# RWKV-5 time mixing and a SwiGLU block: chunks of 64 tokens with one score product per head, and y with channels on partitions

## The chip, the core and the metric

The kernel runs on one core of one Trainium2 chip. A core has a matrix engine (PE; its weight loads are shown as PEld), three engines for elementwise work (DVE, ACT, POOL) and SP, which issues the transfers here. Each takes its instructions in order. The metric is the device time of one execution in microseconds.

## What is computed

Time mixing over 4 batches, 8 heads, 768 tokens and 48 channels, then a feed-forward block with an RMS norm over 3,072 tokens, 384 features and 1,536 hidden units. Everything is float32, except that the three weight matrices arrive as float64.

```python
state = np.zeros((B, H, D, D), dtype=np.float32)
for t in range(S):
    kt, vt, rt = (k[:, :, t], v[:, :, t], r[:, :, t])
    cur = np.einsum('bhd,bhe->bhde', u[None] * kt, vt)
    y[:, :, t] = np.einsum('bhd,bhde->bhe', rt, state + cur)
    state = w[None, :, :, None] * state + np.einsum('bhd,bhe->bhde', kt, vt)
x = np.ascontiguousarray(y.transpose(0, 2, 1, 3)).reshape(B * S, H * D)
xn = x / np.sqrt(np.mean(x * x, axis=-1, keepdims=True) + 1e-06) * rms_g
g = xn @ w_gate
out = (g * (1.0 / (1.0 + np.exp(-g))) * (xn @ w_val)) @ w_out
```

`w` is drawn between 0.85 and 0.95.

## The kernel before

**Time mixing** goes chunk by chunk: 128 tokens of one batch, 24 chunks. `r` and `k` lie with channels on partitions, two heads to a tile (rows 0-47 and 64-111). The scores A[t,j] = sum of r[t] k[j] w^(t-1-j) over j < t are built in seven levels (halves of 64, 32, ..., 1 tokens), so that no power of w is negative: `prep` (L253) multiplies k by falling powers on POOL (L259) and r by rising ones on DVE (L264), `levels` (L279) has one product for each level and head (L292), even heads into one PSUM bank and odd heads into the other, and DVE copies the masked part of each level into `AT` (L300; the largest half by ACT, L297). `outputs` (L308) forms r.(uk) (L315), k-hat times v for the state (L322), r w^t times the state (L329) and A times v (L335), adds them on DVE and takes the sum of squares on ACT. The result has tokens on partitions.

**Feed-forward** works on blocks of three chunks, 384 tokens. `transposes` turns x (L378); `gate_val` (L386) makes for each of 12 hidden tiles two products of three matmuls (L393), a sigmoid on ACT (L397) and two multiplications on DVE (L398, L399); `project` (L401) adds 12 products for 128 tokens (L406) and ACT copies the result out (L410). Matmuls in float32 appear as two passes, so as two records.

**Weights** are rounded to float32 in 36 pieces of 128 x 384 by `round_piece` (L161): six operations on DVE (L176 to L187) and an addition on POOL (L188). `rounded` puts this ahead of the first product that needs a piece.

**Order.** The source interleaves steps of the feed-forward part of the block before (`todo`, `step`) with the mixing of the present chunk; a scheduler then fixes each engine's order from dependences, priorities and free buffers. PSUM has two tiles for the levels, two for gate and value and two for all else (projections among it).

Of the kernel before, what the change touches and what calls it, by code (L numbers as in the profile page):

```python
# [13 lines left out]
"""  # L14
# [14 lines left out]
FP32 = mybir.dt.float32  # L29
# [4 lines left out]
ALU = mybir.AluOpType  # L34
PSUM = bass.MemoryType.PSUM

P = 128
L = 128
EPS = 1e-6


def free_dims(t, *dims):
# [5 lines left out]
def tile_rwkv5_then_swiglu(  # L48
    ctx: ExitStack,
    tc: tile.TileContext,  # L50
    rT: bass.AP,  # [B, H, D, S]
    kT: bass.AP,  # [B, H, D, S]
    k: bass.AP,  # [B, S, H, D]
    v: bass.AP,  # [B, S, H, D]
    w: bass.AP,  # [H, D]
    u: bass.AP,  # [H, D]
    w_gate: bass.AP,  # [DM, DFF]
    w_val: bass.AP,  # [DM, DFF]
    w_out: bass.AP,  # [DFF, DM]
    rms_g: bass.AP,  # [DM]  # L60
    out: bass.AP,  # [B * S, DM]
):
    nc = tc.nc

# [11 lines left out]
    WQ = 4  # L76
# [59 lines left out]
    # The weights in float32. Given in float64 (its bits, as int64), they are rounded here, piece by piece.  # L136
# [67 lines left out]
    # masks[s][j, q, i]: whether j is in the left half of block q (of 2s tokens), whose right half's tokens are i  # L204
# [13 lines left out]
    # powers of w by doubling: up[n] = w^n, down[n] = w^(L-1-n), wL = w^L  # L218
# [14 lines left out]
    # w^(L-1-t) with tokens on partitions  # L233
# [19 lines left out]
    def prep(n):  # L253
        """What chunk n needs of r, k and the powers of w."""
# [24 lines left out]
    def levels(n, two):  # L279
        """A^T of chunk n for one or two sizes of halves; one bank for the even heads, one for the odd."""  # L280
# [27 lines left out]
    def outputs(n):  # L308
        """Chunk n's rows of x, the sums of their squares, and the next state."""
# [131 lines left out]
    while todo:  # L441
        step()


# [26 lines left out]
```

## Time and profile before

| | us |
|---|---|
| median of three runs | 947.51 (947.07 to 949.36) |
| span of the profiled execution, first to last instruction | 943.5 |
| gate products L393 (pg), busy | 217.6 |
| value products L393 (pv), busy | 201.6 |
| projections L406, busy | 198.9 |
| score products L292, busy | 164.2 for the levels by R and K |
| masked copies L300 on DVE, busy | 130.5 |
| powers times k, L259 on POOL, busy | 125.7 |

The page gives a span; the execution's own time is not listed apart from the runs', and 4.0 us lie between its span and their median. A row of a group reads: line, engine, operation, output and inputs by the program's names, tile shapes, count, then busy us, the mean of one in ns, and the idle time ahead of them with what ended it. In the timeline a row is a run of equal instructions: start, duration, engine, line, operation, count, and in brackets a wait ahead of it. In the slices a digit is a busy share in tenths.

### The profile page before, as it was taken

The numbers are of one execution on the slowest core, as the hardware profiler recorded it, in microseconds if no ns is written. First come the engines' busy times: TensorE is split into PE (matmuls) and PEld (weight loads), VectorE is DVE, ScalarE is ACT, GpSimd is POOL, SyncE is SP. The second block draws the span as 40 slices with busy tenths as digits, with TensorE's granted clock in tenths as the row PEclk, the third lists the DMA queues.
The fourth block names the chain that finished last, engine by engine and source line by source line (L and its number), as shares of the span: only waits on it lengthen the run. The fifth ranks groups of instructions, "written<-read, shape, count | busy, mean of one in ns | idle before, by whom it ended". The sixth has DMA issues, their size and how long they took to land.

```text
span 943.5 us, 13386 instructions
## 1 busy us (share of the span) xinstructions
PE 897.9 (95%) x5548; PEld 619.5 (66%) x5548; DVE 483.1 (51%) x874; ACT 121.9 (13%) x241; POOL 241.4 (26%) x291
## 2 busy tenths in 40 slices
PE   4776999979999999999999999999999999999998
PEld 4776766646667667766667667766667667766554
DVE  8999999972454435542455334542455334431220
ACT  0000211001211121101211121101211121102110
POOL 9864544450123112211123112211123110000000
PEclk9999999968999999999999999999999999999999
DMA  7343333110100101100100101100100100000000
GB/s 210 109 120 107 86 91 101 56 46 25 52 14 21 43 17 34 34 17 26 43 25 19 42 17 34 34 17 28 41 17 9 35 18 1 1 1 26 1 0 26
DMA packets 36556, 38.81 MB, mean 41 GB/s; under 512 B 4112, under 2 KB 31888, under 8 KB 36496
## 3 DMA queue, kind: packets, MB, share of 16 engines
q1 hardware_dynamic: 36496, 37.96, 14.0%
q8 instruction: 44, 0.72, 0.3%
q14 instruction: 16, 0.13, 0.0%
HBM read 33.23 MB, written 4.72 MB: 40 GB/s over the span
## 4 chain that ended last, share of the span: by engine, by line
PE 82%; DVE 13%; POOL 2%; issue 1%; DMA 1%; ACT 0%; SPq 0%; POOLq 0%; ACTq 0%; DVEq 0%
PE pg L393 20%; PE po L406 20%; PE pv L393 18%; PE pp L292 14%; PE Y L335 4%; PE Y L329 3%; DVE AT L300 2%; PE su L315 2%; DVE R L264 1%; DVE t L187 1%; PE su L322 1%; DVE t L182 1%; DVE t L186 1%; PE px L378 1%; POOL wo L188 1%
## 5 line engine op out<-in xcount | busy, mean ns | idle before, releaser
L393 PE MATMUL pg<-xT,wg 128*128 128x384 f32 x576 | 217.6, 516 | 2.1 <-DVE h L398 2.1
L406 PE MATMUL po<-wo,h 128*128 128x384 f32 x576 | 198.9, 501 | 6.1 <-POOL wo L188 5.7
L393 PE MATMUL pv<-xT,wv 128*128 128x384 f32 x576 | 201.6, 486 | 0.0
L259 POOL TENSOR_TENSOR K<-kT,down 128x256 f32<-128x256 f32 x144 | 125.7, 882 | 276.2 <-PE pp L292 271.3
L292 PEld LDWEIGHTS pp<-R,K 48*128 48x128 f32 (+1 forms) x2304 | 149.0, 201 | 59.4 <-issue 44.3
L292 PE MATMUL pp<-R,K 48*128 48x64 f32 (+1 forms) x2304 | 164.2, 291 | 18.6 <-DVE AT L300 16.6
L406 PEld LDWEIGHTS po<-wo,h 128*128 128x128 f32 x576 | 109.0, 194 | 80.2 <-POOL wo L188 8.4
L393 PEld LDWEIGHTS pv<-xT,wv 128*128 128x128 f32 x576 | 109.8, 191 | 77.3 <-issue 1.4
L393 PEld LDWEIGHTS pg<-xT,wg 128*128 128x128 f32 x576 | 106.1, 196 | 64.7 <-issue 6.6
L300 DVE COPY_PREDICATED AT<-mask,pp 128x512 f32<-128x512 int32 x144 | 130.5, 906 | 34.8 <-PE pp L292 28.3
L398 DVE TENSOR_TENSOR h<-pg,h 128x384 f32<-128x384 f32 x96 | 53.4, 557 | 139.5 <-ACT h L397 139.4
L264 DVE TENSOR_TENSOR R<-rT,up 128x256 f32<-128x256 f32 x144 | 66.9, 480 | 83.7 <-PE pp L292 82.9
L397 ACT ACTIVATE h<-pg 128x384 f32<-128x384 f32 x96 | 47.2, 491 | 337.1 <-PE pg L393 331.6
L399 DVE TENSOR_TENSOR h<-pv,h 128x384 f32<-128x384 f32 x96 | 53.4, 556 | 66.6 <-PE pv L393 66.6
L335 PE MATMUL Y<-v,AT 128*128 128x48 f32 x384 | 60.4, 289 | 3.1 <-DVE AT L300 3.1
L335 PEld LDWEIGHTS Y<-v,AT 128*128 128x128 f32 x384 | 56.8, 215 | 4.6 <-DVE AT L300 3.4
L275 POOL TENSOR_TENSOR khat<-k,wk 128x384 f32<-128x384 f32 x20 | 21.5, 1076 | 148.3 <-PE su L322 148.3
L329 PE MATMUL Y<-S,Rin 128*128 128x96 f32 x160 | 38.0, 323 | 0.0
L271 POOL TENSOR_TENSOR Rin<-rT,up 128x512 f32<-128x512 f32 x20 | 26.2, 1310 | 38.9 <-PE Y L329 38.0
L410 ACT COPY o<-po 128x384 f32<-128x384 f32 x24 | 11.5, 479 | 189.8 <-PE po L406 189.8
L297 ACT COPY AT<-pp 64x512 f32<-64x512 f32 x24 | 13.9, 581 | 151.9 <-PE pp L292 151.9
L315 PEld LDWEIGHTS su<-u,rk 128*128 128x128 f32 x192 | 28.2, 214 | 7.6 <-DVE rk L273 2.0
(69 smaller groups left out, 496.1 us busy)
## 6 DMA issues: line engine op xcount, KB each, us to landing
k<-in_k_dram SPq DMA_DIRECT2D x24, 192.0 KB, 2.4
kT<-in_kT_dram SPq DMA_DIRECT2D x48, 96.0 KB, 2.3
rT<-in_rT_dram SPq DMA_DIRECT2D x48, 96.0 KB, 2.5
v<-in_v_dram SPq DMA_DIRECT2D x24, 192.0 KB, 2.4
raw<-in_w_gate_dram SPq DMA_DIRECT2D x12, 384.0 KB, 3.8
raw<-in_w_val_dram SPq DMA_DIRECT2D x12, 384.0 KB, 3.8
raw<-in_w_out_dram SPq DMA_DIRECT2D x12, 384.0 KB, 3.1
out_dram<-o SPq DMA_DIRECT2D x24, 192.0 KB, 1.9
```

Of the source, the lines that this page charges most:

```text
L259: nc.gpsimd.tensor_mul(halves(kd, s, 0) if s < L // 2 else kd.rearrange("p a (q s) -> p a q s", s=s), halves(k_, s, 0), free_dims(down[:, ...
L264: nc.vector.tensor_mul(Rs[s][n % 2].rearrange("p a (q s) -> p a q s", s=s), halves(r_, s, 1), free_dims(up, (L, HP), (0, q), (1, s)),)
L292: nc.tensor.matmul(pp[0:M, e * HP + hc, i, :], lhsT, rhs, start=True, stop=True, skip_group_check=True)
L300: nc.vector.copy_predicated(halves(AT, s, 1), free_dims(masks[s], (0, H), (s, q), (1, s)), pp[:, :, i, :].rearrange("p a (q s) -> p a q s" ...
L315: nc.tensor.matmul(du[:, 2 * hc : 2 * hc + 2], rk[n][:, hc, :], u2[:, hc, :], start=True, stop=True, skip_group_check=True)
L329: nc.tensor.matmul(Y[:, 2 * hc : 2 * hc + 2, :].rearrange("p a d -> p (a d)"), R_in[n][:, hc, :], Sb[:, hc, :], start=True, stop=False, sk ...
L335: nc.tensor.matmul(Y[:, h, :], AT[:, e * HP + hc, :], vn[:, h * D : (h + 1) * D], start=c == 0, stop=True, skip_group_check=True,)
L393: nc.tensor.matmul(ps_, wt[:, cc, o * P : (o + 1) * P], xT[:, cc, :], start=cc == 0, stop=cc == CC - 1)
L397: nc.scalar.activation(h, pg, AF.Sigmoid)
L398: nc.vector.tensor_mul(h, pg, h)
L399: nc.vector.tensor_mul(h, pv, h)
L406: nc.tensor.matmul(po, hT[nn][:, j * P : (j + 1) * P], wo[i][:, o, :], start=nn == 0, stop=nn == NN - 1)
```

## The change

A new function `fast` does all of the work where each w lies in 0.5 to 1.5; the kernel of before stays as `general`, behind a branch on a count of the channels in that range.

* A chunk is 64 tokens of **all four batches**: 12 chunks. Powers of w are centred: r is multiplied by w^(t-32) and k by w^(31-j), so one product of 48 x 64 by 64 per head and batch gives all scores. Even heads use rows 0-47 and write partitions 64-127, odd heads the reverse; both go to one PSUM bank.
* `ME` (even heads) and `MO` (odd) hold r w^t in 48 rows and the scores in the other 64, with r.(uk) put on the diagonal by POOL. `VS` holds the state in the same 48 rows and v in the other 64. One product over 128 rows gives y with **channels on partitions**, so the transposes go. The fourth pair of heads is spread over rows 48-63 and 112-127 of the three feature tiles, by products of its own into the same columns.
* `KH` holds the diagonal of w^64 and k-hat, so one product gives the next state; ACT copies it into the next `VS`.
* The mean of squares comes from a product with a matrix of ones, over 256 tokens.
* Feed-forward blocks are 256, 256, then five times 512 tokens.
* Weights come in 24 pieces of 128 x 576: four operations on DVE, one on ACT, one on POOL.
* PSUM: four tiles for gate and value, three for mixing, one for projections.

```diff
+    ps_gv = ctx.enter_context(tc.tile_pool(name="ps_gv", bufs=4, space=PSUM))
+    ps_at = ctx.enter_context(tc.tile_pool(name="ps_at", bufs=3, space=PSUM))
+    ps_o = ctx.enter_context(tc.tile_pool(name="ps_o", bufs=1, space=PSUM))
...
+    def round_piece():
...
+            nc.scalar.activation(ulp, lo, AF.Copy, scale=2.0**-29)
+            mi = mag.bitcast(I32)
+            nc.vector.tensor_single_scalar(out=mi, in_=hi, scalar=0x7FFFFFFF, op=ALU.bitwise_and)
+            nc.vector.tensor_single_scalar(out=mag, in_=mag, scalar=2.0**-15, op=ALU.max)
+            nc.vector.tensor_scalar(
+                out=mi, in0=mi, scalar1=3, scalar2=0x3FFFFFF8, op0=ALU.logical_shift_left, op1=ALU.bitwise_and
+            )
+            nc.vector.scalar_tensor_tensor(
+                out=mi, in0=hi, scalar=-0x40000000, in1=mi, op0=ALU.bitwise_and, op1=ALU.bitwise_or
+            )
+            nc.gpsimd.tensor_tensor(out=dst.bitcast(I32), in0=mi, in1=ulp, op=ALU.add)
...
+    def prep(s):
...
+        nc.vector.tensor_mul(kc, ch[:, 1], table(down))
+        nc.vector.tensor_mul(me[0:D], ch[0:D, 0], table(up[0:D]))
+        nc.vector.tensor_mul(mo[64 : 64 + D], ch[64 : 64 + D, 0], table(up[64 : 64 + D]))
+        if s + 1 < NS:
+            load_chan(s + 1)
+        rk = one.tile([P, B, HP, D], FP32, name=f"rk_{s}", tag="rk")
+        nc.gpsimd.tensor_mul(rk, TOK[:, 0], TOK[:, 1])
+        nc.gpsimd.tensor_mul(rk, rk, free_dims(utab, (0, B), (D, HP), (1, D)))
+        du = work.tile([P, B * HP], FP32, name=f"du_{s}", tag="du")
+        nc.vector.tensor_reduce(out=du, in_=rk.rearrange("p b h d -> p (b h) d"), op=ALU.add, axis=AX.X)
+        for t, rows in ((me, slice(64, 128)), (mo, slice(0, 64))):
+            nc.gpsimd.tensor_mul(
+                t[rows].rearrange("p b h t -> p (b h) t"),
+                free_dims(dmask[rows], (0, B * HP), (1, L)),
+                free_dims(du[rows], (1, B * HP), (0, L)),
+            )
...
+    def scores(s, half):
...
+                for rows, to, m in ((slice(0, D), slice(64, 128), me), (slice(64, 64 + D), slice(0, 64), mo)):
+                    nc.tensor.matmul(
+                        pa[to, bl, p, :], kc[rows, b, p, :], m[rows, b, p, :], start=True, stop=True,
+                        skip_group_check=True,
+                    )
+        for to, m in ((slice(64, 128), me), (slice(0, 64), mo)):
+            nc.vector.copy_predicated(
...
+    def outputs(s, half):
...
+                for z, m in ((0, me), (1, mo)):
+                    nc.tensor.matmul(
+                        py[64 * z : 64 * z + 64, i, cols], vs[:, z, b, at : at + L], m[:, b, 3, :],
+                        start=True, stop=False, skip_group_check=True,
+                    )
+                for z, m in ((0, me), (1, mo)):
+                    nc.tensor.matmul(
+                        py[64 * z : 64 * z + D, i, cols], vs[:, z, b, i * D : (i + 1) * D], m[:, b, i, :],
+                        start=False, stop=True, skip_group_check=True,
+                    )
...
+        nc.scalar.activation(sq_of[s][:, :, cols], py, AF.Square)
+        nc.scalar.copy(yT_of[s][:, :, cols], py)
+        if half == 1:
+            sq = sq_of[s]
+            nc.gpsimd.tensor_add(sq[:, 0], sq[:, 0], sq[:, 1])
+            nc.gpsimd.tensor_add(sq[:, 0], sq[:, 0], sq[:, 2])
...
+    def states(s, half):
...
+                    nc.tensor.matmul(
+                        pu[64 * z : 64 * z + D, bl, p, :], KH[:, z, b, p, :], vh, start=True, stop=True,
+                        skip_group_check=True,
+                    )
...
+    def normalise(s, xT, at):
+        pm = ps_at.tile([P, B * L], FP32, name=f"pm_{s}", tag="at")
+        nc.tensor.matmul(pm, ones, sq_of[s][:, 0], start=True, stop=True)
+        rms = one.tile([P, B * L], FP32, name=f"rms_{s}", tag="rms")
+        nc.scalar.activation(rms, pm, AF.Sqrt, scale=1.0 / DM, bias=eps)
+        nc.vector.reciprocal(rms, rms)
+        for i in range(CC):
+            nc.vector.scalar_tensor_tensor(
+                out=xT[:, i, at : at + B * L], in0=yT_of[s][:, i], scalar=gcol[:, i : i + 1], in1=rms,
...
+    def project(blk, j, s):
+        rounded(6 * WQ)
+        po = ps_o.tile([P, DM], FP32, name=f"po_{blk}_{j}", tag="po")
...
+    blocks = [[0], [1]] + [[s, s + 1] for s in range(2, NS, 2)]
...
+    in_range = nc.values_load(ok[0:1, 0:1], min_val=0, max_val=P * HP)
+    with tc.If(in_range < P * HP):
+        rT, kT, k, v, w_gate, w_val, w_out, rms_g = general_args
+        general(tc, rT, kT, k, v, w, u, w_gate, w_val, w_out, rms_g, out)
```

Three places of PE's order show what moves. First a stretch of a full block, before: value and gate products (`pv`, `pg`) with two levels of scores (`pp`) between them.

```order
L393 MATMUL pv_8_3119<-xT_2803,wv_126 128x384 x3
L292 MATMUL pp_64_3138<-R_0_214,K_0_246 64x64 x8
L292 MATMUL pp_64_3138<-R_0_216,K_0_226 128x64 x8
L393 MATMUL pg_9_3157<-xT_2803,wg_123 128x384 x3
L393 MATMUL pv_9_3158<-xT_2803,wv_127 128x384 x3
L292 MATMUL pp_16_3169<-R_0_218,K_0_230 128x64 x8
L292 MATMUL pp_16_3169<-R_0_220,K_0_234 128x64 x8
```

The same kind of place now: `pu` are the states, `py` the outputs (of even heads by `ME`, of odd by `MO`).

```order
L408 MATMUL pg_4_1551<-xT_1182,wg_119 128x512 x3
L408 MATMUL pv_4_1552<-xT_1182,wv_123 128x512 x3
L371 MATMUL pu_0_1563<-VS_90,KH 48x48 x16
L337 MATMUL py_0_1584<-ME_92,VS_90 64x64
L337 MATMUL py_0_1584<-MO_94,VS_90 64x64
L342 MATMUL py_0_1584<-ME_92,VS_90 48x64
L342 MATMUL py_0_1584<-MO_94,VS_90 48x64
```

All products of the mixing have at most 64 output rows now, and the two column halves of the array alternate; the wide products are 512 long.

Second, the first projection (`po`), before:

```order
L406 MATMUL po_0_1509<-wo_130,h_8_1281 128x384
L292 MATMUL pp_16_1613<-R_0_220,K_0_234 128x64
L406 MATMUL po_0_1509<-wo_131,h_9_1330 128x384
L406 MATMUL po_0_1509<-wo_131,h_10_1386 128x384
L329 MATMUL Y_1530<-S_256,Rin_1129 128x96
```

and now:

```order
L422 MATMUL po_0_899<-wo_128,h_8_663 128x384
L408 MATMUL pg_3_1013<-xT_916,wg_119 128x256 x3
L408 MATMUL pv_3_1014<-xT_916,wv_123 128x256 x3
L337 MATMUL py_0_1077<-ME_92,VS_90 64x64
L337 MATMUL py_0_1077<-MO_94,VS_90 64x64
L422 MATMUL po_0_899<-wo_129,h_9_745 128x384
L342 MATMUL py_0_1077<-ME_92,VS_90 48x64
```

The tenth product (with `h_9`) is the first to need the last group of weights, `wo_129`. Before it now stand the first block's gate and value products, four pairs of the second block's and the mixing of chunks 0, 1 and part of 2; everything else of PE is behind it.

Third, two projections of one block, before:

```order
L406 MATMUL po_1_3315<-wo_130,h_8_3126 128x384
L406 MATMUL po_1_3315<-wo_131,h_9_3165 128x384
L406 MATMUL po_1_3315<-wo_131,h_10_3213 128x384
L406 MATMUL po_1_3315<-wo_131,h_11_3244 128x384
L292 MATMUL pp_64_3339<-R_1_217,K_1_227 128x64 x8
```

and now, with the mean of squares (`pm`) and the next chunk's first two scores (`pa`) between them:

```order
L422 MATMUL po_2_1948<-wo_129,h_11_1789 128x384
L388 MATMUL pm_1965<-sq_1876,ones 128x256
L314 MATMUL pa_0_2042<-ME_92,kc_2014 64x64
L314 MATMUL pa_0_2042<-MO_94,kc_2014 64x64
L422 MATMUL po_3_1973<-wo_126,h_0_1457 128x384
```

The next projection now uses the one tile that the last one has filled; in the last block nothing at all lies between them.

More of the change, by code (lines that the diff above doesn't have):

```diff
@@ L34, with feature_order @@
 ALU = mybir.AluOpType
+AX = mybir.AxisListType
 PSUM = bass.MemoryType.PSUM
 P = 128
-L = 128
 EPS = 1e-6
+W_LOW, W_HIGH = 0.5, 1.5
 def free_dims(t, *dims):
     return bass.AP(tensor=t.tensor, offset=t.offset, ap=[list(t.ap[0])] + [list(d) for d in dims])
-@with_exitstack
-def tile_rwkv5_then_swiglu(
+B, H, S, D = 4, 8, 768, 48
+HP = H // 2
+L = 64
+NS = S // L
+DM, DFF = H * D, 1536
+CC = DM // P
+NN = DFF // P
+WQ = 4
+NQ = NN // WQ
+VC = 3 * D + 3 * L
+def feature_order():
+    rows = []
+    for i in range(CC):
+        for z in range(2):
+            rows += [(2 * i + z) * D + d for d in range(D)]
+            rows += [(6 + z) * D + 16 * i + d for d in range(16)]
+    return rows
@@ L49, in tile_rwkv5_then_swiglu, with general @@
+@with_exitstack
+def general(
     ctx: ExitStack,
@@ new lines, in program @@
+def program(ctx, tc, fast_args, general_args, w, u, out):
+    nc = tc.nc
+    flags = ctx.enter_context(tc.tile_pool(name="flags", bufs=1))
+    ok = flags.tile([1, 1], I32, name="ok")
+    chan, tok, vpad, wgt, wvl, wot, g_cols = fast_args
+    fast(tc, chan, tok, vpad, w, u, wgt, wvl, wot, g_cols, out, ok)
+    in_range = nc.values_load(ok[0:1, 0:1], min_val=0, max_val=P * HP)
+    with tc.If(in_range < P * HP):
+        rT, kT, k, v, w_gate, w_val, w_out, rms_g = general_args
+        general(tc, rT, kT, k, v, w, u, w_gate, w_val, w_out, rms_g, out)
```

334 lines of the change are left out of this document (318 added, 16 removed).

## The prediction

> **What bounds the kernel now.** First the page: engines and slices.
>
> ```profile
> span 943.5 us, 13386 instructions
> PE 897.9 (95%) x5548; PEld 619.5 (66%) x5548; DVE 483.1 (51%) x874; ACT 121.9 (13%) x241; POOL 241.4 (26%) x291
> ...
> PE   4776999979999999999999999999999999999998
> ...
> DVE  8999999972454435542455334542455334431220
> ```
>
> PE is full from about 220 us on; before that DVE is, and PE has holes. So there are two stages with different limits. Four windows show the change from one to the other (columns: window, length, then busy us and instructions of PE, PEld, DVE, ACT, POOL, then the granted clock, the DMA share and GB/s):
>
> ```profile
> 10.00:20.00 10.00, 7.04 (x61) 6.43 (x61) 9.08 (x18) 0.58 (x1) 10.00 (x14) 1.00 0.97 292
> 20.00:30.00 10.00, 5.02 (x55) 4.74 (x54) 10.00 (x13) 0.00 (x0) 10.00 (x11) 1.00 0.52 110
> ...
> 180.00:200.00 20.00, 16.17 (x113) 10.56 (x114) 18.23 (x38) 0.49 (x1) 8.76 (x8) 0.94 0.26 79
> ...
> 400.00:500.00 100.00, 100.00 (x653) 68.24 (x650) 42.64 (x72) 14.02 (x27) 18.23 (x22) 1.00 0.10 27
> ```
>
> Then the chain in order of time, which in the second stage is PE alone and gives its period:
>
> ```profile
> 218.61 17.10 PE po L406 x48
> ...
> 311.16 7.94 PE po L406 x24
> ...
> 841.47 7.94 PE po L406 x24
> ...
> 916.86 23.23 PE po L406 x72
> ```
>
> From 311.16 to 841.47 lie five blocks of 384 tokens: 106.1 us each. What PE does in one is read from its timeline (start, duration; I take the distance of starts, since durations overlap; a float32 matmul is two passes, two records):
>
> ```profile
> 571.68 0.95 PE L315 MATMUL su<-u,rk 128*128 128x2 f32 x8
> 572.56 0.67 PE L322 MATMUL su<-v,khat 128*64 128x48 f32 x16
> 573.16 0.46 PE L329 MATMUL Y<-S,Rin 128*128 128x96 f32 x2
> ...
> 577.88 2.10 PE L393 MATMUL pv<-xT,wv 128*128 128x384 f32 x6
> 579.91 1.72 PE L292 MATMUL pp<-R,K 48*64 48x64 f32 x32
> 581.56 2.20 PE L393 MATMUL pg<-xT,wg 128*128 128x384 f32 x6
> 583.60 2.10 PE L393 MATMUL pv<-xT,wv 128*128 128x384 f32 x6
> 585.63 2.00 PE L292 MATMUL pp<-R,K 48*128 48x64 f32 x32
> 587.56 2.20 PE L393 MATMUL pg<-xT,wg 128*128 128x384 f32 x6
> ...
> 872.19 2.10 PE L393 MATMUL pv<-xT,wv 128*128 128x384 f32 x6
> 874.13 2.10 PE L393 MATMUL pg<-xT,wg 128*128 128x384 f32 x6
> ```
>
> Six passes of 384 columns take 1.94 us: 0.323 us a pass, 0.84 ns a column. So the feed-forward part costs 1,728 x 0.323 = **558 us**, or 69.8 us a block. The remaining 36.3 us of a block are the time mixing of three chunks: 12.1 us each, 24 x 12.1 = **290 us**. Span less both is 943.5 - 558 - 290 = **95 us**, what the DVE-bound start loses.
>
> **The change, part by part.** *Feed-forward.* Columns before: 1,728 x 384 = 663,552. After: 288 passes of 256, 720 of 512 and 576 of 384 are 663,552 too. At 0.84 ns a column nothing changes: 558 us. A 512 pass (0.430) and a 256 pass (0.215) are not in the trace; both ends of the scaling, with or without a few ns a pass, differ by under 5 us.
>
> *Mixing.* The seven levels of scores become one, and `u` and `R_in` go into the one output product. Passes after: scores 768 (48 rows x 64 columns, 64 moving), outputs 1,152 (128 x 64 or 48, 64 moving), states 704 (128 x 48, 48 moving), means 24 of 256. The rows above give: pp 48*128 1.93/32 = 60 ns a pass; the 32 passes at 579.91 are sixteen of 48*64 and sixteen of 48*128, so 1.65 - 0.97 leaves 43 ns for 48*64; su L322 (128*64) 0.60/16 = 37.5 ns; su L315, full width and nothing beside it, 0.88/8 = 110 ns. Scores 768 x 43 = 33; outputs, between L322 and 48*64, at the dearer 43: 49.5; states at 37.5: 26.4; means 5.2. Each turn between wide and narrow passes costs some 0.1 us (the six passes at 577.88 take 2.03 in place of 1.94); six more a chunk are 7. Sum **121 us** for 290. Unknown stays the price of the narrow passes: half of 60 would give 91, all of 60 gives 169.
>
> The Trainium skill, "TensorEngine Tiling (Array Packing)", Gotcha 1, says that different row tiles must not use one PSUM bank at the same time. Before, the two row halves go to two banks; `scores` now sends them to two halves of the partitions of one. By that rule the scores would lose their neighbour (rival B); no row here shows the case.
>
> *The start.* Weights come as float64 and are rounded on DVE, POOL and now ACT. Rows by form:
>
> ```profile
> L300 DVE COPY_PREDICATED AT<-mask,pp 128x512 f32<-128x512 int32 x144 | 130.5, 906 | 34.8 <-PE pp L292 28.3 <-ACT AT L297 6.2
> ...
> L271 POOL TENSOR_TENSOR Rin<-rT,up 128x512 f32<-128x512 f32 x20 | 26.2, 1310 | 38.9 <-PE Y L329 38.0
> ...
> L187 DVE SCALAR_TENSOR_TENSOR t<-raw,t 128x384 f32<-128x384 uint32 x36 | 23.6, 656 | 0.0
> ...
> L273 DVE TENSOR_TENSOR rk<-rT,kT 128x512 f32<-128x512 f32 x24 | 20.0, 834 | 22.3 <-PE su L315 22.2
> L182 DVE TENSOR_SCALAR t<-raw 128x384 int32<-128x384 int32 x36 | 19.7, 549 | 4.8 <-POOL wo L188 4.8
> ...
> L97 POOL MEMSET K<- 128x512 f32 x10 | 4.7, 524 | 0.0
> ```
>
> A piece is now 576 wide and takes three TENSOR_SCALARs and one SCALAR_TENSOR_TENSOR: (3 x 549 + 656) x 1.5 = 3.45 us, 83 us for 24. These means hide two levels:
>
> ```profile
> 21.50 1.08 DVE L187 SCALAR_TENSOR_TENSOR t<-raw,t 128x384 f32<-128x384 uint32 x1
> 22.50 0.88 DVE L182 TENSOR_SCALAR t<-raw 128x384 int32<-128x384 int32 x1
> ...
> 144.82 0.35 DVE L176 TENSOR_SCALAR wv<-raw 128x384 int32<-128x384 int32 x1
> 145.09 0.55 DVE L187 SCALAR_TENSOR_TENSOR t<-raw,t 128x384 f32<-128x384 uint32 x1
> ```
>
> With POOL at work a piece would be 5.6 us, with POOL idle 2.4 (the same operations at 21.5 and at 145 us, times 1.5). POOL's own work in this stage, 21 additions of 576 columns and the products of three chunks, is some 75 of 110 us at 2.56 ns a column, so neither end holds throughout; I keep 3.45, the mean of a stage of the same kind.
>
> The first chunk hangs on POOL's queue: memsets of 11,000 columns at 1.02 ns are 11.3 us, constants 4, then 7 products (two for KH's diagonal, two for `rk`, two for KH's other rows: 768 wide; `ME`'s diagonal: 1,024) at 2.56 ns: 14.4, and `MO`'s 2.6. So MO is ready at 33 us. Behind it on DVE: four predicated copies and three rounding steps, 6 us. PE then does 160 passes at half speed (below), 86 ns: started beside the copies, done at 48. Squares, two adds on POOL, the mean, root, reciprocal and three scalings take 6: the feed-forward starts at **54 us**. From there DVE owes 21 pieces (72.5), eight 1,024-wide products of `prep` (8 x 1.67 = 13.3), eight copies (7.2), 28 products of 256 (10.4) and 6 of small ones: 109. POOL's last add makes it **165 us** when the last weights are ready. PE stands in its queue at the tenth product of the first projection (the second place of the order shown with the change): it has done chunks 0 and 1, a part of 2, and 192 + 18 feed-forward passes, 72 us of 558 + 121. **607 us** remain.
>
> *After it.* The projections have one PSUM tile where they had two. In the last block three follow their predecessor directly, so PE waits for ACT's copy (0.48 and the handing over, 0.8); at five more places only 0.6 us of other work lies between. A gap also costs clock:
>
> ```profile
> 27.71 3.68 PE L292 MATMUL pp<-R,K 48*128 48x64 f32 x32 [4.98 <-DVE AT L300]
> ...
> 146.25 3.87 PE L393 MATMUL pg<-xT,wg 128*128 128x384 f32 x6 [0.70 <-DVE h L398]
> 149.96 2.10 PE L393 MATMUL pv<-xT,wv 128*128 128x384 f32 x6
> ```
>
> After 0.70 us without work six passes take 3.71 us, 1.8 more than elsewhere (at 27.71 it is 105 ns a pass for 60). So 3 x 2.6 and five small ones: **12 us**. "TensorE: Matmul & The Clock Gate" of the Trainium skill, Part 1, has the clock fall after an idle window of about 3.4 us. By it these gaps would cost 4 us, not 12. The trace disagrees: 0.70 us was enough.
>
> The copies, additions and table loads of ACT, DVE and POOL lie beside PE's 50 to 60 us a chunk: DVE owes some 20 of them, POOL 15, ACT 13. If that cover went, each chunk would pay the wait for its means, about 3 us (two adds, a table load and a root). The loads of a chunk are 2.3 MB in five transfers on SP's queue: 7.7 us at the 292 GB/s of the second window, beside 50; those that the first chunk waits for, 1.6 MB, are there at some 9 us, ahead of POOL's chain. In the start SP issues them in one queue with the weights, and the order puts a chunk's channels behind pieces that wait for a free buffer: a delay there would come on top of the 165 us, and I put it at nothing because DVE has five to nine rounding operations to do meanwhile.
>
> *The end.* After the last matmul before:
>
> ```profile
> 940.16 0.48 ACT L410 COPY o<-po 128x384 f32<-128x384 f32 x1 [7.26 <-PE po L406]
> ```
>
> From there to 943.5 are 3.3 us. Each engine then loads the count of channels in range and branches past the general path; no row shows that: nothing at best, 10 us by my guess at worst, I take 3.
>
> Sum: 165 + 607 + 12 + 3.3 + 3 = 790 us of span. The runs' median lies 4.0 us above the span (947.5 against 943.5): **794 us**.
>
> **The rivals.** *B, scores one by one:* 768 passes at 110 instead of 43 ns add 51: 845. For it speaks the shared bank; against it L322, whose two column halves share one tile and still cost 37.5. *C, a slower start:* with pieces at 5.6 us, 21 x 2.15 = 45 more: 839. The first 40 us before look so; from 100 us on they don't. *D, all cheaper:* pieces at 2.4 take 22 off, narrow passes at 30 ns another 30: 742. *E, slower than before:* all 2,624 narrow passes at L315's 110 ns, 180 us more: **974**. It decides from 43 + 153/2,624, about 100 ns a pass. Against it stand L322 and the 48*64 rows; outputs alone have both a full row range and 64 moving columns, which no row has. *F, gaps in the steady stage:* two a chunk for ten chunks at 2.5 us: 844; DVE's share of 40% speaks against it. *G, the branch doesn't skip:* all of the old work follows, about 1,740. Every w lies in 0.85 to 0.95, inside the range tested.
>
> **How the numbers follow.** Forecast 0.60, B 0.10, C 0.12, D 0.08, F 0.04, E 0.05, G 0.01. The range has to take in B, C and F and the price of the passes upwards, and half of D downwards: 752 to 850. A measurement of this kernel tells 0.3% (2.8 us) from no change: faster 0.94, same 0.01, slower 0.05.
>
> **What would show it.** Scores and outputs near 43 ns a pass between starts; PE without holes from about 165 us; rounding groups near 0.9 us an operation; the first feed-forward product near 54 us; 0.8 us waits of PE for ACT at L422 in the last block, with a half clock behind each; no instruction of the general path in the trace. Outputs at 100 ns, or DVE full beyond 200 us, would prove me wrong.

## The result and the profile after

| | us |
|---|---|
| before, median of 4 runs beside it | 948.2 (947.07 to 949.36) |
| after, median of 4 runs | 764.57 (763.41 to 766.71) |
| ratio after/before | 0.8068, 95% interval 0.8052 to 0.8083 |
| span of the profiled execution after | 761.7 |
| forecast | 794 (752 to 850) |

The change makes the kernel a fifth faster, and the forecast was 29 us too high. First the page after (engines, three rows of the slices, the chain by engine):

```profile
span 761.7 us, 9960 instructions
PE 680.2 (89%) x4238; PEld 389.6 (51%) x4238; DVE 338.9 (44%) x435; ACT 154.9 (20%) x307; POOL 220.3 (29%) x141
...
PE   2465667788999999999999999999999999999994
...
DVE  7769889827444362244461433460433420222200
...
PEclk9968979999999999999999999999999999999998
...
PE 66%; POOL 13%; DVE 13%; issue 3%; DMA 3%; ACT 1%; POOLq 0%; ACTq 0%; DVEq 0%
```

PE's digits are 8 from the ninth slice on (152 us) and 9 from the eleventh (190 us); before, PE was full from 220 us. Ahead of that, DVE and POOL have their high digits, and a quarter of the chain is theirs. The windows (columns as in the prediction) put numbers to the two stages:

```profile
46.00:156.00 110.00, 76.06 (x583) 56.88 (x582) 96.38 (x137) 27.62 (x54) 60.41 (x36) 0.87 0.48 139
...
300.00:400.00 100.00, 99.05 (x613) 52.00 (x608) 41.00 (x44) 22.34 (x45) 28.71 (x16) 1.00 0.19 46
...
600.00:700.00 100.00, 99.82 (x404) 50.66 (x403) 24.15 (x36) 13.83 (x23) 1.45 (x2) 1.00 0.04 8
```

Where the start ends is read from the timeline of POOL, whose last addition of weights is this:

```profile
153.31 1.40 POOL L194 TENSOR_TENSOR wo<-mag,ulp 128x576 int32<-128x576 int32 x1
```

So the last weights are ready at 154.7 us, for 165 forecast. The mixing is read from PE's timeline in the second stage. First scores, then a group of states (pu) and outputs (py) between two projections:

```profile
290.37 0.22 PE L314 MATMUL pa<-ME,kc 48*64 48x64 f32 x1
290.38 0.22 PE L314 MATMUL pa<-MO,kc 48*64 48x64 f32 x1
290.43 0.22 PE L314 MATMUL pa<-ME,kc 48*64 48x64 f32 x1
290.44 0.22 PE L314 MATMUL pa<-MO,kc 48*64 48x64 f32 x1
...
291.34 8.01 PE L422 MATMUL po<-wo,h 128*128 128x384 f32 x24
299.28 0.92 PE L371 MATMUL pu<-VS,KH 128*48 128x48 f32 x32
...
301.52 8.01 PE L422 MATMUL po<-wo,h 128*128 128x384 f32 x24
```

Passes come in pairs: the one for an odd head starts less than 10 ns behind the one for an even head, and the next pair 0.06 us (58 to 59 ns) after the last. That is 29.5 ns a pass, where the forecast had 43. Thirty-two states and 48 outputs take 2.24 us, 28 ns a pass; the 32 scores end in a projection at 291.34. A chunk of two such halves costs some 7 us and half a microsecond for its mean, against 10.1 in the forecast (121 over 12).

What PE waits for, by form (columns: line, engine, operation, tiles, shapes, count, busy us and mean ns, idle time ahead and what ended it):

```profile
L422 PE MATMUL po<-wo,h 128*128 128x384 f32 x576 | 195.6, 495 | 12.3 <-POOL wo L194 10.3 <-ACT o L426 2.0
L408 PE MATMUL pg<-xT,wg 128*128 128x512 f32 x360 | 167.4, 599 | 1.2 <-DVE xT L393 0.7 <-DVE h L414 0.3
...
L408 PE MATMUL pg<-xT,wg 128*128 128x256 f32 x144 | 43.2, 432 | 13.2 <-POOL wg L194 8.8 <-DVE xT L393 4.3
L408 PE MATMUL pv<-xT,wv 128*128 128x256 f32 x144 | 39.1, 408 | 12.9 <-POOL wv L194 12.9
...
L388 PE MATMUL pm<-sq,ones 128*128 128x256 f32 x24 | 8.7, 448 | 8.7 <-POOL sq L355 8.7
```

Weights (10.3, 8.8 and 12.9 us behind POOL's additions) are the larger part, and no such wait outlasts the start; the means wait 8.7 us for the sums of squares, 4.4 of it in the first chunk.

### The profile page after: what moved, and what is told of

Same layout as the page of the kernel before. It is cut to its first block, busy times and chain, and to the rows that moved or that the text cites. A ratio compares the mean times of both kernels' runs of the same rounds, so it can differ in the third digit from the quotient of the medians.

```text
span 761.7 us, 9960 instructions
## 1 busy us (share of the span) xinstructions
PE 680.2 (89%) x4238; PEld 389.6 (51%) x4238; DVE 338.9 (44%) x435; ACT 154.9 (20%) x307; POOL 220.3 (29%) x141
## 4 chain that ended last, share of the span: by engine, by line
PE 66%; POOL 13%; DVE 13%; issue 3%; DMA 3%; ACT 1%; POOLq 0%; ACTq 0%; DVEq 0%
PE pg L408 21%; PE pv L408 20%; PE po L422 17%; POOL KH L301 4%; DMA TOK<-in_tok_dram 3%; DVE xT L393 3%; PE pa L314 2%; PE pu L371 2%; POOL rk L285 2%; POOL rk L286 2%; DVE mag L191 2%; DVE mag L186 2%; PE py L337 1%; DVE mag L187 1%; PE py L342 1%
## 5 line engine op out<-in xcount | busy, mean ns | idle before, releaser
L408 PE MATMUL pg<-xT,wg 128*128 128x512 f32 (+1 forms) x504 | 210.6, 552 | 14.3 <-POOL wg L194 8.8
L408 PE MATMUL pv<-xT,wv 128*128 128x512 f32 (+1 forms) x504 | 203.4, 540 | 12.9 <-POOL wv L194 12.9
L422 PE MATMUL po<-wo,h 128*128 128x384 f32 x576 | 195.6, 495 | 12.3 <-POOL wo L194 10.3
L301 POOL TENSOR_TENSOR KH<-TOK,wk 64x768 f32<-64x768 f32 x22 | 47.0, 2137 | 244.0 <-PE pu L371 243.2
L414 DVE TENSOR_TENSOR h<-pg,h 128x512 f32<-128x512 f32 (+1 forms) x84 | 51.4, 612 | 145.1 <-ACT h L413 144.9
L413 ACT ACTIVATE h<-pg 128x512 f32<-128x512 f32 (+1 forms) x84 | 45.0, 536 | 287.7 <-PE pg L408 286.5
L415 DVE TENSOR_TENSOR h<-pv,h 128x512 f32<-128x512 f32 (+1 forms) x84 | 51.5, 613 | 70.0 <-PE pv L408 69.0
L337 PE MATMUL py<-ME,VS 128*64 128x64 f32 x288 | 36.7, 231 | 2.5 <-DVE ME L319 2.0
L337 PE MATMUL py<-MO,VS 128*64 128x64 f32 x288 | 36.7, 231 | 1.5 <-DVE MO L319 1.5
L342 PE MATMUL py<-MO,VS 128*48 128x64 f32 x288 | 36.2, 227 | 0.0
L342 PE MATMUL py<-ME,VS 128*48 128x64 f32 x288 | 36.2, 227 | 0.0
```

The lines of the kernel that those rows point to most:

```text
L301: nc.gpsimd.tensor_mul(KH[rows, z], TOK[rows, 1], free_dims(wk[rows], (0, B), (D, HP), (1, D)))
L337: nc.tensor.matmul(py[64 * z : 64 * z + 64, i, cols], vs[:, z, b, at : at + L], m[:, b, 3, :], start=True, stop=False, skip_group_check=True,)
L342: nc.tensor.matmul(py[64 * z : 64 * z + D, i, cols], vs[:, z, b, i * D : (i + 1) * D], m[:, b, i, :], start=False, stop=True, skip_group_c ...
L408: nc.tensor.matmul(ps_, wt[:, cc, o * P : (o + 1) * P], xT[:, cc, 0:nt], start=cc == 0, stop=cc == CC - 1)
L413: nc.scalar.activation(h, pg, AF.Sigmoid)
L414: nc.vector.tensor_mul(h, pg, h)
```

## The experiments

Differences of a few us between two kernels need a floor, so the changed kernel ran a second time, on the chip and in the rounds of three of the others.

**The changed kernel again.** No edit.

> The changed kernel once more, unaltered, on the chip and in the rounds of the three runs beside it: within 2 us of 764.6, and the start (last weights ready at 154.7 us) within 3 us. What differs between the two is the floor under which no difference of the neighbours is told as one.

Measured: 767.12 us (ratio to before 0.8091, 0.8074 to 0.8109), last weights at 156.9 us. That is 2.5 us above the first measurement, slightly more than expected: what differs by less than that isn't told as a difference below. The run beside a kernel is this one for the three that say so (sign on ACT, squares on DVE, first block of 512); against the first measurement their gains are 2.5 us smaller.

**Every score twice.**

```diff
-                for rows, to, m in ((slice(0, D), slice(64, 128), me), (slice(64, 64 + D), slice(0, 64), mo)):
+                for rows, to, m in 2 * ((slice(0, D), slice(64, 128), me), (slice(64, 64 + D), slice(0, 64), mo)):
```

> Every score product is issued twice into the same place (768 more narrow passes), nothing else is changed; the output stays the reference's. Theory: two neighbouring passes on the two halves of the array take 59 ns together, as the spacing of 7 and 52 ns in the changed kernel's trace has it, and TensorE has no idle time after the start to hide them: 704 of the 768 lie behind the start, so +21 us (about 785). Rival, the price of my prediction (43 ns for each pass): +30 us or more (about 795). Second rival, that the passes lie beside other work or that TensorE was idle: under +5 us.

Measured: 787.2 us (0.8317, 0.8301 to 0.8334), +22.6. The count in the expectation was off: three chunks, not one, have their scores done before the last weights are ready, so 576 added passes lie behind that point. From the last weights to the last projection's end the trace has 614.2 us where the changed kernel has 597.3 and, in its second run, 598.6. That is 27 to 29 ns a pass; 43 ns would make 24.8 us. The rest came in the start, whose end moved from 154.7 to 158.9. So the price is near 29.5 ns, and there is no idle PE that would hide it.

**Even heads first, then odd.** In `scores`, and likewise in `outputs`, the loop over the two halves becomes the outer one:

```diff
-        for bl in range(2):
-            b = 2 * half + bl
-            for p in range(HP):
-                for rows, to, m in ((slice(0, D), slice(64, 128), me), (slice(64, 64 + D), slice(0, 64), mo)):
+        for rows, to, m in ((slice(0, D), slice(64, 128), me), (slice(64, 64 + D), slice(0, 64), mo)):
+            for bl in range(2):
+                b = 2 * half + bl
+                for p in range(HP):
```

> The same passes in another order: in a group of scores or outputs all passes of the even heads first, then all of the odd heads, so that neighbours no longer go to different halves; states stay as they are. Theory (29 ns a pass comes from two neighbours running beside each other): a pass then takes 52 to 59 ns by itself, 1,760 passes behind the start get 23 to 30 ns dearer, +40 to +53 us (805 to 818). Rival (29 ns is what a pass costs by itself): within 3 us of 764.6.

Measured: 791.94 us (0.8374, 0.8353 to 0.8394), +27.4: between the two, on the side of the theory. Two views of this run say why it isn't 40. Its timeline has a group of 32 scores from 358.32 to 360.15:

```profile
358.32 0.97 PE L314 MATMUL pa<-ME,kc 48*64 48x64 f32 x13
...
360.15 2.84 PE L407 MATMUL pg<-xT,wg 128*128 128x512 f32 x6
```

1.83 us for 32, where the same group took 1.08 us from 290.26 (its first pass) to 291.34. Passes on one half follow each other at 56 to 58 ns, twice 29.5; only where the group changes from even to odd heads do some run beside each other. Outputs that follow each other now also add into one place, but scores don't, and they got dearer alike. By the distances of starts, scores and outputs behind the last weights take 77 us where they took 42. But fewer of them than expected, 1,464, lie there, and PE waits less:

```profile
L387 PE MATMUL pm<-sq,ones 128*128 128x256 f32 x24 | 7.2, 383 | 2.2 <-POOL sq L354 2.2
```

The means' wait of 8.7 us has become 2.2, and that of the value products for weights fell from 12.9 to 8.3. Since the gaps for the means, the two stretches at half clock and a few passes no longer lie behind the last weights (159.3), 23 us of the 35 are left from there to the last projection; the start ended 4.6 later. So alternating the halves is what makes a pass cost 29.5 ns.

Rival B fails too. In the kernel before, the two halves of the 48*64 scores went to two banks, and inside the group at 579.91 us neighbours start 6 to 7 and 51 to 52 ns apart by turns; now, in one bank, they do the same. By "TensorEngine Tiling (Array Packing)" of the Trainium skill, Gotcha 1, different row tiles can't use a bank at the same time; the rows at 290.37 have them less than 10 ns apart, and no cost of it shows.

**Without the guard for tiny weights.**

```diff
-            nc.vector.tensor_single_scalar(out=mag, in_=mag, scalar=2.0**-15, op=ALU.max)
```

> The second of VectorE's four operations on each piece of weights (the guard for tiny weights, line 187, 685 ns in the mean) is left out; weights below it would be rounded wrongly. Theory: VectorE paces the start, and 24 x 0.685 us = 16 us less of its work brings the last weights forward by 10 to 14 us, and the end by as much (about 752). Rival: GpSimd's additions, the transfers or the waits between VectorE and ScalarE pace the start: 3 us or less.

Measured: 753.58 us (0.7965, 0.7945 to 0.7984), -11.0. POOL's last addition of weights, by the timeline:

```profile
142.51 1.40 POOL L193 TENSOR_TENSOR wo<-mag,ulp 128x576 int32<-128x576 int32 x1 [3.01 <-DVE mag L190]
```

It ends at 143.9, 10.8 us sooner, and the end of the kernel moves by the same. DVE paces the start. That 16 us of work left out give 11 has two parts in the trace: up to the last weights DVE is busy 14.0 us less (128.6 to 114.6), as some of its other operations got dearer (L191, here L190: 884 to 965 ns in the mean) and one cheaper (L186: 901 to 800), and it is idle 2.1 us more (25.7 to 27.8).

**The sign on ACT.** The same, with nothing left out:

```diff
-            nc.vector.tensor_single_scalar(out=mi, in_=hi, scalar=0x7FFFFFFF, op=ALU.bitwise_and)
+            nc.scalar.activation(mag, hi.bitcast(FP32), AF.Abs)
```

> The first of VectorE's four operations on each piece of weights (clearing the sign, line 186, 901 ns in the mean) is done as an absolute value by ScalarE instead; nothing is left out. Theory (VectorE paces the start, ScalarE has time: 38 of its first 156 us are busy): the end comes forward as by leaving out line 187, -8 to -14 us (751 to 757). Rival: ScalarE's additional 0.9 us a piece stand ahead of its other work in the start, and the chain through ScalarE gets as long as the one through VectorE: within 3 us.

Measured: 759.57 us (0.802, 0.8000 to 0.8039): 7.5 below the changed kernel in the same rounds, just under the expected 8 to 14 (5.0 below the first measurement). The last weights are ready at 148.1 us, 8.9 sooner than in the run beside it. DVE keeps waits for ACT (2.7 us), and its three other operations on a piece get dearer (L187, L188 and L191: 2.35 to 2.68 us together). Why is not shown.

**Squares added on DVE.**

```diff
-            nc.gpsimd.tensor_add(sq[:, 0], sq[:, 0], sq[:, 1])
-            nc.gpsimd.tensor_add(sq[:, 0], sq[:, 0], sq[:, 2])
+            nc.vector.tensor_add(sq[:, 0], sq[:, 0], sq[:, 1])
+            nc.vector.tensor_add(sq[:, 0], sq[:, 0], sq[:, 2])
```

> The two additions of squares for the means go from GpSimd to VectorE. Theory: the waits of the means' products for them go (8.7 us in all, one of 3.2 us followed by 3.4 us at half clock), and VectorE has room behind the start: -3 to -6 us (about 760). Rival: VectorE, which paces the start, gets 8 additions more there and gives it back: within 2 us, or up to 3 us slower.

Measured: 765.62 us (0.8085, 0.8069 to 0.8100), 1.5 below the run beside it: no difference. The rival holds, and both halves of it show:

```profile
L408 PE MATMUL pg<-xT,wg 128*128 128x512 f32 (+1 forms) x504 | 211.6, 554 | 19.6 <-DVE xT L393 8.0 <-POOL wg L194 8.0 <-DVE h L414 3.6
...
L388 PE MATMUL pm<-sq,ones 128*128 128x256 f32 x24 | 8.0, 415 | 3.7 <-DVE sq L355 3.7
```

The means' wait falls from 8.7 to 3.7, but the last weights come 3 us later than in the run beside it (160.0 against 156.9), and gate products wait 3.6 us for DVE to read their predecessors (h L414), where it was 0.3 (0.6 in the run beside it).

**The first block of 512 tokens.**

```diff
-    for f in mixing(0, 0, 0):
+    for f in mixing(0, 0, 0) + mixing(1, 0, B * L):
...
-    blocks = [[0], [1]] + [[s, s + 1] for s in range(2, NS, 2)]
+    blocks = [[s, s + 1] for s in range(0, NS, 2)]
```

> Chunks 0 and 1 are both mixed before the first block, and the first block has 512 tokens instead of 256; the passes are the same but for 144 wide ones of 256 columns that become 72 of 512. Theory: in the start TensorE waits for pieces of weights (28 us behind GpSimd's roundings in the trace), and a first block of 512 gives it twice the work for each piece that is there: less of the feed-forward is left when the last weights are ready, -10 to -20 us (745 to 755). Rival: the first product comes some 20 us later, and the weights meanwhile aren't rounded any sooner, so that nothing is won or up to 10 us lost.

Measured: 760.17 us (0.8023, 0.8008 to 0.8038), 7.0 below the run beside it (4.4 below the first measurement); the theory had 10 to 20. The timeline of PE shows what is left:

```profile
76.24 2.08 PE L408 MATMUL pg<-xT,wg 128*128 128x512 f32 x2 [3.05 <-DVE xT L393]
...
152.12 1.22 PE L388 MATMUL pm<-sq,ones 128*128 128x256 f32 x2 [13.36 <-POOL sq L355]
```

PE starts the feed-forward 31 us later and doesn't wait for weights at all any more, though they are complete 13 us later (167.7). In place of that a mean stands in PE's queue and waits 13.4 us for two additions, which have their place in POOL's queue among the additions of weights; most of these wait for DVE:

```profile
146.20 0.93 POOL L354 TENSOR_TENSOR sq<-sq 128x256 f32<-128x256 f32 x1
148.19 1.54 POOL L194 TENSOR_TENSOR wo<-mag,ulp 128x576 int32<-128x576 int32 x1 [1.06 <-DVE mag L191]
149.70 2.37 POOL L355 TENSOR_TENSOR sq<-sq 128x256 f32<-128x256 f32 x1
```

**Blocks of 256 throughout.**

```diff
-    blocks = [[0], [1]] + [[s, s + 1] for s in range(2, NS, 2)]
+    blocks = [[s] for s in range(NS)]
```

> The changed kernel with blocks of 256 tokens throughout, as in the kernel before; mixing, branch and all else stay. Theory (a wide pass costs its columns: 216 ns at 256, 429 ns at 512): 720 passes of 512 become 1,440 of 256 at 1.5 ns more for each half, +2 us, and with it the mixing is spread over more places, so that up to 30 more turns between wide and narrow passes come in at 0.25 us, up to +7 us: 765 to 775. Rival (blocks of 512 are what won the time, by half the weight loads): 785 or more.

Measured: 756.58 us (0.7996, 0.7976 to 0.8015): 8 us below the changed kernel. Both sides expected it slower; the larger blocks cost time here. The start is the same (last weights at 154.8). From there to the last projection's end it is 589.7 us where the changed kernel has 597.3. The passes cost the same for their columns (216 ns for 256, 429 for 512). The waits went:

```profile
L408 PE MATMUL pg<-xT,wg 128*128 128x256 f32 x864 | 219.7, 390 | 13.3 <-POOL wg L194 8.8 <-DVE xT L393 4.5
...
L388 PE MATMUL pm<-sq,ones 128*128 128x256 f32 x24 | 7.4, 391 | 4.8 <-POOL sq L355 4.8
```

The means wait 4.8 us, all of it in the start, where the changed kernel has 5 us more behind it: by the distances of starts, one of 3.2 us and three of 0.6. In a block of two chunks the first chunk's mean stands in the middle of the gate and value products, 12 passes behind the outputs that it needs (2.6 us of 256 columns, 5.2 of 512). That isn't enough: at 377.79 us it waits because POOL's two products for `KH` (370.70 to 375.26) stand ahead of the additions of squares. Then its reciprocal and scalings hold DVE ahead of the reading of the gate products. In the changed kernel's timeline:

```profile
384.63 1.74 DVE L391 RECIPROCAL rms<-rms 128x256 f32<-128x256 f32 x1
...
386.41 3.07 DVE L393 SCALAR_TENSOR_TENSOR xT<-yT,gcol,rms 128x256 f32<-128x256 f32 x3
...
390.13 2.84 PE L408 MATMUL pg<-xT,wg 128*128 128x512 f32 x6 [0.26 <-DVE h L414]
```

That is 4.8 us of DVE beside 5.2 us of PE. With one chunk a block the means stand behind projections. So 5 us of waits for the means, 1.7 of half clock behind the longest, 1.3 of gaps ahead of gate products and two of three stalls at the end (1.6) have gone, and dearer pairs of passes (2.2) and more turns (1.1) give 3.3 back. That is 6.3 of the 7.6 us; it is read from two traces, and no run takes one of these parts alone.

**No branch.**

```diff
-    in_range = nc.values_load(ok[0:1, 0:1], min_val=0, max_val=P * HP)
-    with tc.If(in_range < P * HP):
-        rT, kT, k, v, w_gate, w_val, w_out, rms_g = general_args
-        general(tc, rT, kT, k, v, w, u, w_gate, w_val, w_out, rms_g, out)
```

> The value isn't read back and there is no branch and no general path behind it; the count and its product stay. The fall-back for decays outside the bounds is left out. Theory: reading the value on every engine and branching stands behind the last transfer and costs 5 to 6 us (last product's end to the span's end 9.7 us here, 3.3 us in the kernel before): about 759. Rival (the 9.7 us are the last output's transfer): within 1 us.

Measured: 762.62 us (0.8052, 0.8032 to 0.8072), 2.0 and 4.5 below the two measurements with the branch. The tail itself did what the theory said: ACT's last copy starts at 752.04 in a span of 761.7 with the branch, and here at

```profile
758.02 0.48 ACT L426 COPY o<-po 128x384 f32<-128x384 f32 x1 [8.14 <-PE po L422]
```

in a span of 762.1, so 4.1 us instead of 9.6. With the branch, the transfers from 752 us on show two queues that fetch instructions, which are not there without it:

```profile
q14 instruction: 11, 0.09, 2.7%
q8 instruction: 2, 0.03, 1.4%
```

PE's branch instruction lasts from 753.58 to 758.44 us, where those of DVE, ACT, POOL and SP take less than 0.1, so it seems to be PE's that holds the end.

But PE came to its end 6 us later than in the first run of the changed kernel (2.4 later than in the second): the last weights were ready 1.6 us later, and gate products waited 3.6 us for DVE instead of 0.3. Why DVE came to them later without a branch stays open; so the kernel's own gain from it is between nothing and 5 us, though the tail's 5.5 us are shown.

**Three edits together**, the first block of 512, the sign on ACT, and a second buffer for the last block:

```diff
+        last_odd = blk == len(blocks) - 1 and j % 2 == 1
+        po = (ps_at if last_odd else ps_o).tile([P, DM], FP32, name=f"po_{blk}_{j}", tag="at" if last_odd else "po")
-        po = ps_o.tile([P, DM], FP32, name=f"po_{blk}_{j}", tag="po")
```

> Three edits together, nothing left out: chunks 0 and 1 mixed ahead of a first block of 512 tokens; clearing the sign of each piece of weights on ScalarE; and in the last block every second product of the output projection in a buffer of the mixing's, which is idle by then, so that the next product needn't wait for ScalarE's copy. Theory: with the first block of 512 TensorE no longer waits for weights but for the first chunks and for GpSimd's sums of squares, which stand behind the roundings (one gap of 13.5 us at 138 us); fewer VectorE operations bring both forward, and the copies' three gaps of 0.78 us go: 745 to 753 (against 760.2 and 759.6 of the two larger edits alone). Rival: both edits win the same wait, so that together they give no more than the larger one alone: 758 to 760, less 2.3 us for the copies.

Measured: 749.95 us (0.7911, 0.7893 to 0.7929). The two gains add up (7.0, 7.5 and 2.3 for the gaps are 16.8, and it is 17.2 below the second run of the changed kernel), and the three gaps at the end (0.78 us each by the distances of starts) are gone. The long wait for the squares isn't, by PE's timeline:

```profile
144.68 1.22 PE L388 MATMUL pm<-sq,ones 128*128 128x256 f32 x2 [15.80 <-POOL sq L355]
```

**The same without the branch.**

> The same three edits, and the value is neither read back nor branched on (the general path for decays outside the bounds is left out). Theory: the branch costs 5 to 6 us at the end, as the tail of the run without it shows (from the last product's end to the span's end 4.2 us instead of 9.7 us): 5 to 6 us below the run beside it. Rival, by that run's whole time, which fell by only 2 us: 0 to 2 us below it.

Measured: 746.59 us (0.7882, 0.7860 to 0.7903), 3.4 below: between the two. Again the tail is 6 us shorter (10.4 to 4.3 us behind the last projection), and again the last projection ends later (740.6 against 738.7), with 5.8 us of waits for DVE's reading in place of 2.7.

**The same three edits with blocks of 256 behind the first.**

```diff
-    blocks = [[0], [1]] + [[s, s + 1] for s in range(2, NS, 2)]
+    blocks = [[0, 1]] + [[s] for s in range(2, NS)]
```

> As the run with the three edits (first block of 512 tokens, sign on ScalarE, second buffer at the end), but all blocks behind the first have 256 tokens again. Theory, from the run with blocks of 256 throughout: with one chunk for a block the means' products stand behind output products, not behind value products, and no longer wait for the sums of squares (0.60 us for each of four blocks here), nor do gate products wait for VectorE (0.5 to 0.65 us each): 3 to 5 us less than the run with the three edits alone, 745 to 747. Rival (blocks of 256 won their time in the start, where this run is as before): 749 to 751.

Measured: **736.55 us** (ratio to before 0.7773, 0.7760 to 0.7785), 13.4 below the run with the three edits, three times what was expected, and 28 below the changed kernel. Its page, and the means by line:

```profile
span 735.1 us, 11391 instructions
...
PE   2435998899999999999999999999999999999994
```

```profile
L388 PE MATMUL pm<-sq,ones 128*128 128x256 f32 x24 | 8.4, 435 | 7.3 <-POOL sq L355 7.3
```

The theory's mechanism had an effect in a place that it hadn't counted: with one chunk mixed beside the first block, no mean stands in the middle of it, and the wait of 15.8 us at 129 us has gone with those behind the start. The waits for the squares fell from 24.0 to 7.3 us. With one chunk less in the start, though, the last weights are also ready sooner (152.2 us, 160.5 with the three edits), and gate products wait 7.5 us for DVE in place of 2.7; which part of the 13.4 is whose, no run tells. PE is busy for 80% and more from 73 us on, and full from 147 us.

## Why the forecast came out 29 us high

The sum on record was 165 for the start, 607 of remaining work, 12 of waits, and 3.3 and 3 for the end. In the trace after, 154.7 us pass until the last weights are ready, 597.3 from there to the end of the last projection, and 9.7 to the end of the span.

* **What bounds it: right in the main.** Two stages, first DVE and then PE, with PE 99% busy behind the start; leaving out DVE's work brought the end forward by the same 11 us as the last weights. But DVE is not full in the start: it is busy 96.4 us of the 110 from 46 us on.
* **Feed-forward at 0.84 ns a column: right.** 429 ns for 512 columns and 216 for 256. Behind the last weights lie 96 passes of 256, 720 of 512 and 556 of 384 columns: 20.7 + 309 + 180 = 510 us, and the forecast's 607 held 511 of it.
* **Mixing at 121 us: too dear, the largest error.** Its mechanism was right, the size of one term was off: 43 ns a pass for scores and outputs, 37.5 for states. 43 and 37.5 were taken from groups of 16 passes, at whose ends stands a turn to another kind of pass (now 523 ns for the last wide one instead of 429, 149 for the last narrow one instead of 52); the turns were then added a second time. By the distance of neighbours both groups of the kernel before have 29.5 ns. The states now have 23: their products have 48 output rows, where L322 has 64. Of the mixing behind the last weights the forecast had 96 us (607 less 511), and the trace has about 67, an estimate by the distances of starts: 576 scores at 29.5, 914 outputs at 29, 544 states at 23, the means 4 and some 7 for turns. That is 29 us less. The whole comes to some 85 us, below my lower bound of 91.
* **The start at 165: 10 us too late.** The feed-forward began at 45.4, not at 54:

```profile
45.37 1.22 PE L408 MATMUL pg<-xT,wg 128*128 128x256 f32 x2 [2.87 <-DVE xT L393]
```

  The part of the first chunk that failed is PE's. POOL's last product for `MO` ended at 30.1 us (33 in the forecast), but a fifth of the chunk's 160 passes had run by then, and the rest took 53 and then 40 ns, from 36 us on 29, for the forecast's 86: they were done by 37 us instead of 48.

  From the first product to the last weights it is 109.3 us, with 111 forecast, and that is luck in part: the forecast had 109 us of work for DVE and no waits, and the window from 46 us has 96.4 of work and 13.6 without, most of it waits for POOL's `rk`, ACT and PE. A rounded piece took 3.25 us, for 3.45, by DVE's groups of the first 156 us:

```profile
L186 DVE TENSOR_SCALAR mag<-raw 128x576 int32<-128x576 int32 x24 | 21.6, 901 | 2.5 <-DMA raw<-in_wgt_dram 2.5
L191 DVE SCALAR_TENSOR_TENSOR mag<-raw,mag 128x576 int32<-128x576 int32 x24 | 21.2, 884 | 0.1
L188 DVE TENSOR_SCALAR mag<-mag 128x576 int32<-128x576 int32 x24 | 18.7, 779 | 0.1
L187 DVE TENSOR_SCALAR mag<-mag 128x576 f32<-128x576 f32 x24 | 16.4, 685 | 0.1
```
* **The waits at 12: too low, and of another kind.** The stalls of the last block came, but without half clock behind them:

```profile
735.33 8.01 PE L422 MATMUL po<-wo,h 128*128 128x384 f32 x24 [0.61 <-ACT o L426]
743.95 8.01 PE L422 MATMUL po<-wo,h 128*128 128x384 f32 x24 [0.61 <-ACT o L426]
```

  8.62 us lie between them where 24 passes take 7.75: 0.87, for 0.8 forecast, at full rate. The 1.8 us of lost clock that I added for each didn't come. In place of it the means waited, which I had put at nothing because 50 us of PE's work lie beside a chunk; but the means that waited stand in PE's queue at most 12 wide passes (2.6 or 5.2 us) behind the outputs that they need; most of those that didn't wait stand 24 behind (8 us). Behind the last weights PE lost about 20 us in all (597 less 510 and 67): 9 in waits that the rows show, by the distances of starts, some 3.4 in two stretches at half rate (155.2 and 179.1 us), and the rest in shorter gaps and in the error of the other terms.
* **The clock.** The claim that a hole of 0.70 us is enough to halve it didn't hold here: behind the three holes of 0.61 us in the last block there is no half rate. There is one behind a longer hole:

```profile
179.26 1.22 PE L388 MATMUL pm<-sq,ones 128*128 128x256 f32 x2 [3.00 <-POOL sq L355]
180.28 2.55 PE L408 MATMUL pg<-xT,wg 128*128 128x256 f32 x6
182.66 1.46 PE L408 MATMUL pv<-xT,wv 128*128 128x256 f32 x6
```

  Six passes take 2.38 us after it, and 1.30 from 182.66 on. In the granted clock the stretches at half rate are 3.41 us long or multiples of it (13.65 from 39.1 us, 3.41 from 63.0, 10.24 from 104.0, 3.41 from 179.1), and their starts lie on one grid of 3.41 us. "TensorE: Matmul & The Clock Gate" of the Trainium skill, Part 1, describes such a free-running window of 3413 ns. The trace agrees in length and grid. From 39 us on, windows at full rate in which PE was busy for up to 41% were followed by half rate, and those of the last block, with 82%, were not. But a busy share doesn't decide it alone: in the kernel before, the half rate from 146.51 us follows a window whose only hole is the one of 0.70 us (79% busy), and that from 255.74 us follows one in which PE was busy throughout, with short passes. What decides it stays open.
* **The branch at 3: too low.** No run showed that term before; it is 5.5 us in the tail.
* **The range.** Its lower end was to take in half of D, which would be 768; the 752 stated lies four fifths of the way to D. With 768, the measured 764.57 would have been outside.

Together: 10 less in the start, 29 less in the mixing, 8 more in waits, 3.4 more at the end, and the runs' median 2.9 us above the span instead of 4.0: 794 - 10 - 29 + 8 + 3.4 - 1.1 = 765. So 39 us too many and 11 too few stood in the sum, and that they cancel in part is luck. Of the rivals, B fell by the paired rows, C by the start, E and F by the price of the passes and the full windows behind 156 us, and G since nothing of the general path ran. D, all cheaper, was nearest: its 30 ns a pass came, its 22 us from cheaper pieces didn't.

The reckoning that gave 95 us of lost time for the kernel before gives 119 now: the span of 761.7 less 558 of feed-forward and 85 of mixing. Some 89 of them lie in the start (154.7 less 48 of feed-forward and 18 of mixing), 20 behind it and 10 at the end. So the mixing, 85 us for 290, is more than the whole gain.

## What to carry over

Take the price of short matmuls from the distance of neighbours inside a group, and the turn at its ends as a term of its own; and issue neighbours to different halves of the array, since here that is worth half of their price. Ask of each product that an in-order engine has in its queue what stands directly ahead of it: of the 28 us that were still won here, the last 13.4 came with the same products in smaller blocks, with the means elsewhere in PE's queue. Where a first stage is bound by another engine, a larger first block can give PE more work for each piece of weights, as long as nothing in it waits for that engine's queue.

## What the hardware showed that I had not expected

* Two passes of 64 columns on different halves of the array start 6 to 7 ns apart and take 58 to 59 ns as a pair; on the same half each takes 56 to 58 ns by itself. For states, 48 columns and 48 output rows, a pair takes 45 ns; with 48 columns and 64 output rows (L322 before) it is 58 to 59.
* A change from wide to narrow passes costs 0.09 us and the way back 0.10 us.
* The read-back of one value and a branch cost 5.5 us at the end of a kernel, while instructions are fetched; PE's branch instruction lasts 4.9 us of it.
